# Two attentions and two feed-forward blocks on one core: the first batch in an order written out by hand, and pooling moved from VectorE to GpSimd

## The chip, the cores and the metric

The kernel runs on one core of a Trainium2 chip. The metric is the device time of one execution in microseconds (us); lower is better. Engines are named as the profile names them: PE is TensorE (matmul), DVE VectorE, ACT ScalarE, POOL GpSimd, SP the queue that issues most DMAs.

## What is computed

From q, k, v of shape (4 batches, 8 heads, 576, 64), all in float32:

```python
# pooled attention: 4 neighbours averaged, full softmax over 144
q_d = q.reshape(B, H, 144, 4, D).mean(axis=3)      # k_d, v_d alike
out_up = np.repeat(sm_attn(q_d, k_d, v_d), 4, axis=2)
# local attention: a row sees the rows less than 4 away (7 at most)
scores = np.where(np.abs(pos[:, None] - pos[None, :]) < 4, scale * q @ k.T, -1e9)
x = out_up + softmax(scores) @ v                   # as (2304 tokens, 512)
h = np.maximum(np.maximum(x @ w1, x @ w2), x @ w3) # 512 -> 768
x = h @ w_out                                      # 768 -> 512
h = x @ w_in                                       # 512 -> 2048
out = np.maximum(0.01 * h, h) @ w_out2             # 2048 -> 512
```

## The kernel before

The tokens are cut into 8 units u of 288 (NCOL), two to a batch. A program first computes the x of a unit (both attentions) and then its first feed-forward block. The second feed-forward block follows for all tokens, in 5 chunks (L3 and L4); the change leaves it alone.

**Feed-forward of a unit.** `L1_mm(u, m, e)` is 12 matmuls: x and the weights are each split into a high and a low part (xh, xl; a weight's two halves), and three products are summed, high by high first, then xl by high, then xh by low. 18 of these (6 m, 3 e) and then 4 `L2(u, o)` of 18 matmuls make a unit's PU = 22 slots. `L1_post` takes the maximum over e (hm) and splits it in hh (ACT) and hl (POOL).

**Weights.** `split_weight` turns a float32 weight into two parts by two ACT passes (wy, wl), two DVE passes on integers, one more ACT pass (high) and one subtraction (low, on POOL at first, later on DVE). The first block has 24 weights of 128x512. 14 of them (AHEAD) are converted during the first batch's attention, the others during u = 0.

**First batch (units 0 and 1).** Both attentions run on PE, four head pairs h. Pooled attention goes through `ds_pool_qk` (pooling q and k by 4, DVE), `ds_scores` (scores, maximum, exp, reciprocal of the sum), `ds_norm` (POOL), `ds_at` (transposes and copies) and `ds_pv`. Local attention goes through `pl_scores` (blocks of 96 rows by 102 columns; a band of very negative numbers is added first, by a matmul with an identity), `pl_aT`, `pl_pv` and `pl_x`, which adds both and writes xh and xl. `pl_pool_v` pools v on POOL. Unit 0's steps are a list of ten steps per head pair, each head pair one step behind the last; unit 1's are spread over the first 9 slots (U1) of u = 0. `keep_warm` puts matmuls on zeros, 20 at the start and 40 after the list.

**Other batches.** Pooled attention keeps these steps; `ds_stages` spreads seven stages of a head pair over slots (table in the loop over b). Local attention works on 128 rows at a time without PE: an item i is half the heads of a unit, so a unit u needs the items 2u and 2u+1. Each item has 3 chunks c: `qk_mult` (POOL, 128x1344), `qk_reduce` (DVE and ACT), then, one item later, `pv_mult` and `pv_sum` (DVE) into the tile O. The products of POOL and of DVE share one tile name, prod, with three buffers. From slot 9 on, the pieces of local attention are dealt evenly to the slots of L1, and `emit_T(u + 1)`, in the second L2 slot of u, transposes O (ps_x, PE), adds the pooled part (x, DVE) and makes xh (ACT) and xl (DVE) for the next unit.

**Order.** Only SP's order is that of the program text (`manual_schedule(engines={SP})`). On every other engine a scheduler orders the instructions when the program is built; on the chip each engine then works its list off strictly in that order.

Of the kernel before, what the change touches and what calls it, by code (L numbers as in the profile page):

```python
# [43 lines left out]
U1 = 9  # L44
AHEAD = 14
NA = 8
NWARM = (20, 40)
# [5 lines left out]
def local_global_attention_moe_kernel(  # L53
# [69 lines left out]
    for edge in (None, "first", "last"):  # L123
        bd = sup.tile([QB, KB], BF16, name=f"band_{edge}")
        P.memset(bd, 0.0)
        conds = [(1, -1, 0), (-1, 1, KB - QB)]
        if edge == "first":
            conds.append((1, 0, -(FAC - 1)))
        if edge == "last":
            conds.append((-1, 0, KB - FAC))  # L130
        for step, cm, base in conds:
            P.affine_select(
                out=bd, in_=bd, pattern=[[step, KB]], base=base, channel_multiplier=cm,
                compare_op=ALU.is_ge, fill=-(2.0**33),
            )
        bands.append(bd)

# [10 lines left out]
    def split_weight(raw, stage, lo_engine):  # L148
# [7 lines left out]
        A.activation(out=l3, in_=low16, func=AF.Copy, scale=2.0**-13, bias=-0.5 + 2.0**-14)  # L156
        V.scalar_tensor_tensor(  # L157
            out=l3, in0=high, scalar=-(2**31), in1=l3, op0=ALU.bitwise_and, op1=ALU.bitwise_or
        )
        V.scalar_tensor_tensor(  # L160
            out=y, in0=y, scalar=3, in1=l3, op0=ALU.logical_shift_left, op1=ALU.bitwise_or
        )
        r = pool.tile([128, 1024], F32R, tag=name, bufs=1, name=name)
        hi, lo = r[:, 0:512], r[:, 512:1024]
        A.activation(out=hi, in_=y.bitcast(F32), func=AF.Copy)
        lo_engine.tensor_tensor(out=lo, in0=y.bitcast(F32), in1=hi.bitcast(F32), op=ALU.subtract)
        return hi, lo
# [16 lines left out]

    def conv_w1(t):
        r = split_weight(wr.pop(t), mmp, P if 1 not in pools else V)
        if t[0] == "A":
            wA[t[1:]] = r
        else:
            wO[t[1]] = r  # L190
# [151 lines left out]
    def pl_load(what, h):  # L342
# [8 lines left out]
        elif what in "01":  # L351
            t = sup.tile([KB, NBLK, 128], F32, tag="sv" + what, bufs=4, name="sv" + what)
            nc.sync.dma_start(out=t.rearrange("p n d -> p (n d)"), in_=vW[0, int(what), h])
        else:
            t = late_tile([QC, 2, 2, FAC, D], "dsrawv")
# [4 lines left out]
    def pl_pool_v(h):  # L360
        raw = dst.pop((0, h, "vr"))
# [6 lines left out]
    def pl_scores(u, h, hh):  # L368
        qr, kr = pl[h, "q"], pl[h, "k"]
        pst = ps_early.tile([QB, 512], F32, tag="early", name="ps_ls")  # L370
        ps = pst[:, : NBLK * KB].rearrange("p (n k) -> p n k", n=NBLK)
        st = pst[:, NBLK * KB :]
        rows = slice(64 * hh, 64 * hh + 64)
# [12 lines left out]
        if hh == 0:
            if u == 0:
                pl[u, h, "e"] = late_tile([QB, 2, NBLK, KB], "ple")
            else:
                pl[u, h, "e"] = sup.tile([QB, 2, NBLK, KB], F32, tag="ple", bufs=2, name="ple")  # L390
        e = pl[u, h, "e"][:, hh]
        for j in range(NBLK):
            A.activation(
                out=e[:, j], in_=ps[:, j], func=AF.Exp, scale=SCALE,
                bias=nm[:, j : j + 1], accum_out=sm[:, j : j + 1],
            )
        if hh == 1:
            e, sm = pl[u, h, "e"], pl.pop((u, h, "sum"))
            sp = st[:, NBLK : 3 * NBLK].rearrange("p (x n) -> p x n", x=2)
            V.tensor_scalar(out=sp, in0=sm, scalar1=1e-9, scalar2=None, op0=ALU.add)  # L400
            V.reciprocal(out=sm, in_=sp)
            for x in range(2):
                (P if u == 0 else V).tensor_tensor(
                    out=e[:, x], in0=e[:, x], in1=sm[:, x].unsqueeze(2).to_broadcast((QB, NBLK, KB)), op=ALU.mult
                )

    def pl_aT(u, h):
# [23 lines left out]
    def pl_x(u, h):  # L431
# [38 lines left out]
    def ds_pool_qk(b, h):  # L470
# [10 lines left out]
    def ds_scores(b, h, hh):  # L481
        t = dst[b, h, "qk"]
        if hh == 0:
            if b:
                dst[b, h, "e"] = small(b, [QC, 2, 2, SD], "dse")
            dst[b, h, "sum"] = pools[b].tile([QC, 4], F32, tag="dssum", bufs=2, name="dssum")
        pst = ps_at.tile([QC, 512], F32, tag="at", name="ps_sc")
        ps = pst[:, : 2 * SD].rearrange("p (c s) -> p c s", c=2)
        st = pst[:, 2 * SD : 2 * SD + 2]
        rows = slice(64 * hh, 64 * hh + 64)  # L490
        for c in range(2):
            T.matmul(out=ps[:, c, :], lhsT=t[rows, 0, c * QC : c * QC + QC], rhs=t[rows, 1, :], start=True, stop=True)
        nm = pools[b].tile([QC, 2], F32, tag="dsnm", bufs=2, name="dsnm")
        V.tensor_reduce(out=st, in_=ps, axis=AX.X, op=ALU.max, negate=True)
        V.tensor_scalar(out=nm, in0=st, scalar1=SCALE / 16.0, scalar2=None, op0=ALU.mult)
        e, sm = dst[b, h, "e"], dst[b, h, "sum"]
        for c in range(2):
            A.activation(
                out=e[:, hh, c, :], in_=ps[:, c, :], func=AF.Exp, scale=SCALE / 16.0,
                bias=nm[:, c : c + 1], accum_out=sm[:, 2 * hh + c : 2 * hh + c + 1],  # L500
            )
        sm, sp = sm[:, 2 * hh : 2 * hh + 2], pst[:, 2 * SD + 2 : 2 * SD + 4]
        V.tensor_scalar(out=sp, in0=sm, scalar1=1e-9, scalar2=float(FAC), op0=ALU.add, op1=ALU.mult)
        V.reciprocal(out=sm, in_=sp)
# [444 lines left out]
```

## Time and profile before

| | |
|---|---|
| three timed runs | 913.1, 913.62 and 914.03 us, median 913.62 |
| the profiled execution | 914.8 us, its span 913.0 us |
| PE busy | 860.4 us, 94% |
| DVE, ACT, POOL busy | 526.8, 412.8 and 247.7 us |
| mean granted clock of PE | 0.932 |
| DMA | 75.13 MB, mean 82 GB/s |

The span is what the profile shows from the first instruction to the last; the execution's own time has 1.8 us more around it. [...]

### The profile page before, as it was taken

Reading aid. Unit: us, or ns where it says so; the run is one execution under the profiler, and the core shown is the slowest. Engines: PE = TensorE matmul, PEld = TensorE weight load, DVE = VectorE, ACT = ScalarE, POOL = GpSimd, SP = SyncE. Lnnn points to the kernel's source line nnn. Section 1 sums busy time; section 2 is a strip of 40 time slices with the busy share of each in tenths; the row PEclk is TensorE's granted clock in tenths of the full one; section 3 lists DMA queues with packets and bytes.
Section 4 is the critical chain, followed back from the end, with each engine's and each line's share of the span. In section 5 each row is a group of like instructions: output and inputs, shape, how many; then the busy total and the mean of one; then the engine's idle time right before and its main releaser. Section 6 shows DMA issues by size and latency. Waiting matters only on the chain.

```text
span 913.0 us, 13518 instructions
## 1 busy us (share of the span) xinstructions
PE 860.4 (94%) x4912; PEld 754.7 (83%) x4914; DVE 526.8 (58%) x919; ACT 412.8 (45%) x1537; POOL 247.7 (27%) x195
## 2 busy tenths in 40 slices
PE   8799988997989989799999999999999999999995
PEld 4478888996978979699999888888887888788894
DVE  3587888887968696777475699242223322322321
ACT  2664754655647456572274687232223222222221
POOL 3553539764755566350111000000000000000000
PEclk9555979897999999799999999999999999999998
DMA  8700624442423133112062920020003000200000
GB/s 219 269 1 24 254 72 147 167 135 70 136 95 122 33 122 111 48 46 73 1 235 105 355 120 1 0 93 1 1 0 93 1 1 2 68 1 1 19 29 23
DMA packets 30132, 75.13 MB, mean 82 GB/s; under 512 B 3267, under 2 KB 8691, under 8 KB 30067
## 3 DMA queue, kind: packets, MB, share of 16 engines
q1 hardware_dynamic: 25459, 69.56, 22.8%
q10 hardware_dynamic: 4608, 4.72, 1.5%
q8 instruction: 38, 0.62, 0.3%
q14 instruction: 27, 0.22, 0.1%
HBM read 64.83 MB, written 9.44 MB: 81 GB/s over the span
## 4 chain that ended last, share of the span: by engine, by line
PE 74%; DVE 12%; DMA 7%; issue 2%; ACT 2%; SPq 1%; POOL 1%; ACTq 0%; POOLq 0%; DVEq 0%
PE ps_h L614 21%; PE acc L717 20%; PE ps_g L693 20%; PE ps_o L644 5%; DMA raw<-x2d 2%; PE ps_up L531 2%; DVE O L298 2%; DVE xl L602 2%; DMA wA<-in_wa_dram 2%; PE ps_ls L379 2%; PE ps_lo L426 1%; DMA sv<-in_vW_dram 1%; DVE wl L157 1%; DVE wy L160 1%; DVE x L594 1%
## 5 line engine op out<-in xcount | busy, mean ns | idle before, releaser
L614 PE MATMUL ps_h<-xh,wA 128*128 128x288 f32 x1152 | 204.5, 311 | 6.3 <-ACT xh L601 3.1
L614 PEld LDWEIGHTS ps_h<-xh,wA 128*128 128x128 f32 x1152 | 177.9, 201 | 9.2 <-ACT xh L601 3.3
L717 PE MATMUL acc<-w2o,gh 128*128 128x512 f32 x576 | 178.2, 391 | 0.9 <-ACT gh L704 0.9
L693 PE MATMUL ps_g<-x2h,w2i 128*128 128x512 f32 (+1 forms) x640 | 158.9, 370 | 0.0
L701 DVE TENSOR_TENSOR g<-g,ps_g 128x512 f32<-128x512 f32 (+1 forms) x80 | 50.7, 634 | 184.0 <-ACT g L700 183.9
L693 PEld LDWEIGHTS ps_g<-x2h,w2i 128*128 128x128 f32 x640 | 114.6, 188 | 22.9
L700 ACT ACTIVATE g<-ps_g 128x512 f32<-128x512 f32 (+1 forms) x80 | 44.3, 553 | 185.2 <-PE ps_g L693 185.1
L614 PE MATMUL ps_h<-xl,wA 128*128 128x288 f32 x576 | 116.5, 308 | 10.7 <-DVE xl L602 10.7
L717 PEld LDWEIGHTS acc<-w2o,gh 128*128 128x128 f32 x576 | 106.8, 188 | 23.7 <-ACT gh L704 1.8
L247 POOL TENSOR_TENSOR qkprod<-lq,lk 128x1344 f32<-128x1344 f32 x36 | 112.0, 3120 | 42.6 <-DVE O L298 25.6
L717 PE MATMUL acc<-w2o,gl 128*128 128x512 f32 x288 | 112.2, 391 | 0.1
L614 PEld LDWEIGHTS ps_h<-xl,wA 128*128 128x128 f32 x576 | 93.2, 199 | 12.9 <-DVE xl L602 11.9
L260 ACT ACTIVATE qkprod<-qkprod 128x64 f32<-128x64 f32 x364 | 87.6, 245 | 24.2 <-POOL qkprod L247 23.8
L693 PE MATMUL ps_g<-x2l,w2i 128*128 128x512 f32 (+1 forms) x320 | 79.6, 370 | 0.0
L644 PE MATMUL ps_o<-hh,wO 128*128 128x288 f32 x384 | 77.4, 298 | 0.0
L705 DVE TENSOR_TENSOR gl<-g,gh 128x512 fp32r<-128x512 f32 (+1 forms) x80 | 51.0, 638 | 39.6 <-ACT gh L704 35.1
L260 ACT ACTIVATION_READ_ACCUMULATOR qkprod<-qkprod 128x1 f32 x364 | 69.6, 191 | 0.0
L704 ACT ACTIVATE gh<-g 128x512 fp32r<-128x512 f32 (+1 forms) x80 | 47.1, 588 | 42.6 <-DVE g L701 42.2
L693 PEld LDWEIGHTS ps_g<-x2l,w2i 128*128 128x128 f32 x320 | 56.8, 188 | 10.9
L635 POOL TENSOR_TENSOR hl<-hm,hh 128x288 fp32r<-128x288 f32 x48 | 40.9, 854 | 88.3 <-ACT hh L634 84.7
L717 PEld LDWEIGHTS acc<-w2o,gl 128*128 128x128 f32 x288 | 54.1, 188 | 12.6 <-DVE gl L705 0.9
L631 DVE TENSOR_TENSOR hm<-hm,ps_h 128x288 f32<-128x288 f32 x96 | 42.3, 445 | 32.8 <-PE ps_h L614 26.9
(124 smaller groups left out, 1216.2 us busy)
## 6 DMA issues: line engine op xcount, KB each, us to landing
wA<-in_wa_dram SPq DMA_DIRECT2D x18, 512.0 KB
w2i<-in_w_in_dram SPq DMA_DIRECT2D x16, 512.0 KB
w2o<-in_w_out_dram SPq DMA_DIRECT2D x16, 512.0 KB
lv<-in_vL_dram SPq DMA_DIRECT2D x12, 480.0 KB
lk<-in_k_dram SPq DMA_DIRECT2D x11, 480.0 KB
dsrawv<-in_vP_dram SPq DMA_DIRECT2D x16, 288.0 KB
x2d<-ev ACTq DMA_DIRECT2D x32, 144.0 KB
raw<-x2d SPq DMA_DIRECT2D x16, 256.0 KB
```

Source lines behind the costliest of these rows:

```text
L247: P.tensor_tensor(out=pr, in0=in0, in1=in1, op=ALU.mult)
L260: A.activation(out=pr[:, r, j], in_=pr[:, r, j], func=AF.Copy, accum_out=sc[:, r, j : j + 1])
L614: T.matmul(out=ps, lhsT=wA[m, e][wi][:, kk * 128 : kk * 128 + 128], rhs=xx[:, kk] if u < PEU else xx[:, :, kk, :], start=n == 0, stop=n == ...
L631: V.tensor_tensor(out=t, in0=t, in1=ps, op=ALU.max)
L635: P.tensor_tensor(out=hl[:, m], in0=t, in1=hh[:, m].bitcast(F32), op=ALU.subtract)
L644: T.matmul(out=ps, lhsT=wO[m][wi][:, os_], rhs=xx[:, m], start=n == 0, stop=n == 3 * M1 - 1)
L693: T.matmul(out=ps, lhsT=w2i[m][wi][:, kk * 128 : kk * 128 + 128], rhs=xx[:, kk, :n], start=j == 0, stop=j == 3 * KC - 1,)
L700: A.activation(out=g, in_=ps, func=AF.Copy, scale=0.01)
L701: V.tensor_tensor(out=g, in0=g, in1=ps, op=ALU.max)
L704: A.activation(out=gh, in_=g, func=AF.Copy)
L705: V.tensor_tensor(out=gl, in0=g, in1=gh.bitcast(F32), op=ALU.subtract)
L717: T.matmul(out=accs[c, t], lhsT=a[:, ts], rhs=w, start=m == 0 and j == 0, stop=m == M2 - 1 and j == 2)
```

## The change

One table (ORDER) sets the order of the first batch on PE, DVE, ACT and POOL; after it the scheduler orders them again. Each step of the pooled and the PE-side local attention is cut into functions of one engine each, named by letters (A is pooling, B, F, G, J, K, M, m, N, v pooled attention, C, D, E, H, I, O, o, P, Q, R, S local attention, L the pooling of v, w x y z u a weight's load and its four conversion steps). Only 8 weights are converted in it, the others follow one per slot of u = 0, all low parts on POOL. Matmuls on zeros (`fill`) stand ahead of most PE steps. A pair of head halves is issued alternately, and one band matmul of 306 columns takes the place of three of 102. `wl3` of these weights lies in PSUM. Unit 1's attention takes slots 0 to 14, local attention of the other batches starts at slot 15 (U1), DONE and TURN set by which slot it ends and where `emit_T` stands (3 to 9 slots ahead of the unit's L1), DS0 and DSOFF where the pooled stages stand. O has two buffers. For batches 1 to 3, q and k are pooled by two additions on POOL, and xl is made on POOL. The loads of v for pooling have 80 rows in place of 72, those for the first batch's local attention 112 in place of 102, the added rows being zeros.

```diff
-U1 = 9
-AHEAD = 14
+U1 = 15
+QP = 80
+KP = 112
+ORDER = (
+    "C0 A0 A1 L0 B0 D0 A2 C1 E0 L1 F0 B1 H0 G0 D1 I0 x0 C2 J0 L2 F1 E1 y0 K0 G1 D2 O0 L3 H1 E2 J1 M0 "
...
+FILL = {"B": 1, "C": 1, "O": 2, "M": 2, "N": 2, "P": 2}
+FILL0 = 20
+FILL1 = 8
+DONE = {2: 39, 3: 59, 4: 79, 5: 100, 6: 121, 7: 142}
+TURN = {2: 41, 3: 62, 4: 82, 5: 103, 6: 124, 7: 145}
+DS0 = {1: (15, 18, 21, 24), 2: (27, 38, 49, 60), 3: (68, 79, 90, 101)}
+DSOFF = {1: (0, 2, 5, 8, 6, 7, 11, 13), 2: (0, 5, 6, 9, 10, 11, 16, 20), 3: (0, 5, 6, 9, 10, 11, 16, 20)}
...
-        l3 = stage.tile([128, 512], I32, tag="wy", bufs=4, name="wl3")
+        l3 = (stage.tile([128, 512], I32, tag="wy", bufs=4, name="wl3") if ps is None else ps()).bitcast(I32)
...
-            O[u] = pools["att"].tile([128, RU, 128], F32, tag="O", bufs=1, name="O")
+            O[u] = pools["att"].tile([128, RU, 128], F32, tag="O", bufs=2, name="O")
...
-            t = sup.tile([KB, NBLK, 128], F32, tag="sv" + what, bufs=4, name="sv" + what)
+            t = sup.tile([KP, NBLK, 128], F32, tag="sv" + what, bufs=4, name="sv" + what)
...
-            V.tensor_reduce(out=t[:, j], in_=dst.pop((b, h, w)), axis=AX.X, op=ALU.add)
+            raw = dst.pop((b, h, w))
+            if b == 0:
+                V.tensor_reduce(out=t[:, j], in_=raw, axis=AX.X, op=ALU.add)
+            else:
+                P.tensor_tensor(out=raw[:, :, 0:2], in0=raw[:, :, 0:2], in1=raw[:, :, 2:4], op=ALU.add)
+                P.tensor_tensor(out=t[:, j], in0=raw[:, :, 0], in1=raw[:, :, 1], op=ALU.add)
...
             A.activation(out=xhf, in_=x32f, func=AF.Copy)
-            V.tensor_tensor(
+            P.tensor_tensor(
                 out=xl[:, g0:g1].rearrange("p r a g -> p (r a g)"), in0=x32f, in1=xhf.bitcast(F32), op=ALU.subtract
             )
...
+    with tc.manual_schedule(engines={ET.SP, ET.PE, ET.DVE, ET.Activation, ET.Pool}):
...
+        fill("", scratch(0, "", "warm_ps"), FILL0)
+        for w in ORDER.split():
+            n = int(w[1])
+            if w[0] in "xyzu":
+                conv_step(W1[n])
+            elif w[0] == "L":
+                pl_pool_v(n)
+            else:
+                if w == "O0":
+                    fill("", scratch(0, "", "warm_ps"), FILL1)
+                steps[w[0]](0, n)
...
+    with tc.manual_schedule(engines={ET.SP}):
...
+        for b in range(1, B):
+            for h in range(4):
+                for off, f in zip(DSOFF[b], ds_stages(b, h)):
+                    at(DS0[b][h] + off, f)
+        for u in range(PEU, NU):
+            at(TURN[u], lambda u=u: emit_T(u))
...
-                    if s == NS + 1 and not last and u + 1 >= PEU:
-                        emit_T(u + 1)
```

**The first batch on PE.** Before, one group of scores of the first batch stands like this (ps_ls are the local scores of one head half, its band and its product for each of three blocks):

```order
L376 MATMUL ps_ls<-band_first,ident_b 96x102
L379 MATMUL ps_ls<-skr,sqr 96x102
L376 LDWEIGHTS ident_b
L376 MATMUL ps_ls<-band_None,ident_b 96x102
L379 MATMUL ps_ls<-skr,sqr 96x102
```

Now the same part of the list has matmuls on zeros (warm) ahead of each step, and both head halves of a pair follow one another (x6):

```order
L166 MATMUL ps_lt<-warm 128x512
L484 MATMUL ps_lt<-ident,ple 102x96 x6
L166 LDWEIGHTS warm
L166 MATMUL ps_ls<-warm 128x512
L421 LDWEIGHTS ident_b
L421 MATMUL ps_ls<-band_108,ident_b 96x306
```

A pair's six band matmuls have become two, and 40 matmuls on zeros stand between the steps, beside 20 at the start and 8 ahead of the first transposes.

**POOL ahead of unit 2's L1.** Before, POOL's list around the end of unit 1 reads (dsrawv and dsv pool v, dse is the normalization, qkprod the local scores' products, hl the low part of h):

```order
L635 TENSOR_TENSOR hl<-hm,hh 128x288
L466 TENSOR_TENSOR dsrawv<-dsrawv 72x4x128
L635 TENSOR_TENSOR hl<-hm,hh 128x288 x2
L509 TENSOR_TENSOR dse<-dse,dssum 72x576
L247 TENSOR_TENSOR qkprod<-lq,lk 128x1344
L467 TENSOR_TENSOR dsv_2372<-dsrawv 72x256
```

Now the list up to unit 2's xl ends like this (dsraw and dsqk pool q and k; the xl of the last row is the first piece of unit 2's):

```order
L291 TENSOR_TENSOR qkprod<-lq,lk 128x1344
L565 TENSOR_TENSOR dsraw<-dsraw 128x144x2 x2
L550 TENSOR_TENSOR dsv_2078<-dsrawv 72x256
L291 TENSOR_TENSOR qkprod<-lq,lk 128x1344
L566 TENSOR_TENSOR dsqk<-dsraw 128x144 x2
L291 TENSOR_TENSOR qkprod<-lq,lk 128x1344
L549 TENSOR_TENSOR dsrawv<-dsrawv 72x4x128
L618 TENSOR_TENSOR dse<-dse,dssum 72x576
L726 TENSOR_TENSOR xl<-x_2253,xh 128x512
```

From the first pooling of q to this xl, POOL's list has 14 qkprod, as many as before up to the same place, and in addition the poolings of q and k; xl stands behind all of them.

**PE at the same place.** Now the end of unit 1 and the start of unit 2 read:

```order
L651 MATMUL ps_up<-aT,dsv_1974 128x144 x4
L577 MATMUL ps_sc<-dsqk 72x144 x4
L697 MATMUL ps_x<-ident,O 128x128 x9
L738 MATMUL ps_h<-xh,wA_0_439 128x288 x4
L738 MATMUL ps_h<-xh,wA_1_454 128x288 x4
L738 MATMUL ps_h<-xh,wA_2_605 128x288 x4
L738 MATMUL ps_h<-xh,wA_0_640 128x288 x4
L629 MATMUL ps_aT<-ident,dse 72x72 x8
L651 MATMUL ps_up<-aT,dsv_2078 128x144 x4
L577 MATMUL ps_sc<-dsqk 72x144 x2
L738 MATMUL ps_h<-xl,wA_0_439 128x288 x4
```

As before the change, four groups of L1 take their xh products first, and the first xl product waits for POOL now, where it waited for DVE.

## Rows read from the trace of the kernel before

**Rows 1.** Busy time by stage: from, to, length; busy us of PE, PEld, DVE, ACT, POOL; clock
```profile
0.00:90.50 90.50, 80.04 (x343) 55.76 (x346) 55.63 (x127) 46.61 (x158) 43.06 (x62) 0.64 0.42 129
90.50:137.80 47.30, 42.43 (x278) 40.01 (x278) 39.94 (x72) 29.66 (x73) 21.93 (x19) 0.86 0.44 165
137.80:222.40 84.60, 75.92 (x531) 71.33 (x529) 69.41 (x124) 43.93 (x256) 63.55 (x36) 0.90 0.38 124
222.40:275.30 52.90, 48.15 (x345) 47.01 (x345) 44.40 (x73) 32.61 (x208) 32.53 (x19) 0.94 0.36 118
275.30:504.20 228.90, 215.95 (x1597) 212.26 (x1598) 161.91 (x276) 119.64 (x593) 86.60 (x60) 0.97 0.28 91
504.20:913.00 408.80, 397.91 (x1824) 328.31 (x1823) 155.46 (x251) 140.37 (x252) 0.00 (x0) 0.99 0.13 44
```

**Rows 2.** Timeline of PE: start, us, instruction; first matmul of L1, and a wait
```profile
90.51 0.59 PE L614 MATMUL ps_h<-xh,wA 128*128 128x288 f32 x1
...
222.38 0.83 PE L614 MATMUL ps_h<-xl,wA 128*128 128x288 f32 x4 [2.38 <-DVE xl L602]
```

**Rows 3.** Timeline of PE in the first batch: matmuls on zeros, then one block's band and scores
```profile
31.36 3.19 PE L784 MATMUL warm_ps<-warm 128*128 128x512 bf16 x7 [0.22 <-issue]
...
85.21 0.32 PE L376 MATMUL ps_ls<-band_None,ident_b 96*96 96x102 bf16 x1
85.46 0.65 PE L379 MATMUL ps_ls<-skr,sqr 64*96 64x102 f32 x2
```

**Rows 4.** DMA from 8 to 15 us, then from 26 to 36 us (weights): packets, rate
```profile
DMA packets 641, 1.44 MB, mean 205 GB/s; under 512 B 70, under 2 KB 179, under 8 KB 641
...
DMA packets 1109, 4.04 MB, mean 404 GB/s; under 512 B 127, under 2 KB 127, under 8 KB 1108
```

**Rows 5.** Timeline of DVE: its first pooling
```profile
3.67 0.75 DVE L478 TENSOR_REDUCE dsqke<-sqr 128x144 f32<-128x576 f32 x1 [2.53 <-DMA sqr<-in_qT_dram]
```

**Rows 6.** Groups on DVE: busy us, mean ns of one | idle before
```profile
L384 DVE TENSOR_REDUCE ps_ls<-ps_ls 96x3 f32<-96x306 f32 x16 | 7.5, 473 | 7.5 <-PE ps_ls L379 7.5
L442 DVE TENSOR_TENSOR x<-ps_lo,up 64x288 f32<-64x288 f32 x16 | 7.2, 453 | 0.5
L504 DVE RECIPROCAL dssum<-ps_sc 72x2 f32<-72x2 f32 x32 | 4.5, 156 | 0.2
L157 DVE SCALAR_TENSOR_TENSOR wl<-wA,wl 128x512 int32<-128x512 int32 x18 | 20.9, 1161 | 11.4 <-ACT wl L156 11.3
L157 DVE SCALAR_TENSOR_TENSOR wl<-w2i,wl 128x512 int32<-128x512 int32 x16 | 10.9, 686 | 3.6 <-ACT wl L156 3.6
```

**Rows 7.** Groups on POOL from 137.8 to 222.4 us
```profile
L247 POOL TENSOR_TENSOR qkprod<-lq,lk 128x1344 f32<-128x1344 f32 x14 | 43.3, 3108 | 2.5 <-DVE O L298 2.4
L466 POOL TENSOR_TENSOR dsrawv<-dsrawv 72x512 f32<-72x512 f32 x5 | 6.4, 1280 | 13.8 <-DMA dsrawv<-in_vP_dram 13.8
L635 POOL TENSOR_TENSOR hl<-hm,hh 128x288 fp32r<-128x288 f32 x8 | 6.4, 805 | 0.3 <-ACT hh L634 0.2
L509 POOL TENSOR_TENSOR dse<-dse,dssum 72x576 f32<-72x576 f32 x4 | 4.6, 1144 | 0.5 <-DVE lp L279 0.5
L467 POOL TENSOR_TENSOR dsv<-dsrawv 72x256 f32<-72x256 f32 x5 | 3.6, 730 | 2.9 <-PE ps_up L531 2.7
```

**Rows 8.** Groups over the whole span: xl on POOL and on DVE, low weight parts, pooling on DVE
```profile
L166 POOL TENSOR_TENSOR wA<-wy,wA 128x512 fp32r<-128x512 f32 x18 | 24.9, 1384 | 23.7 <-ACT wA L165 22.1 <-issue 1.4
L602 DVE TENSOR_TENSOR xl<-x,xh 128x512 fp32r<-128x512 f32 (+3 forms) x18 | 19.9, 1116 | 4.5 <-ACT xh L601 4.5
L478 DVE TENSOR_REDUCE dsqk<-dsraw 128x144 f32<-128x576 f32 x24 | 17.6, 745 | 7.5 <-DMA dsraw<-in_qT_dram 5.9 <-DMA dsraw<-in_kT_dram 1.6
L448 POOL TENSOR_TENSOR xl<-x,xh 128x288 fp32r<-128x288 f32 x8 | 9.0, 1122 | 18.2 <-ACT xh L447 18.2
```

**Rows 9.** Longest waits of POOL from 137.8 to 275.3 us: us in total, times, longest
```profile
POOL dsrawv L466 <- DMA dsrawv<-in_vP_dram: 23.3, 6, 5.8
POOL qkprod L247 <- DVE O L298: 12.5, 3, 6.2
```

More of the change, by code (lines that the diff above doesn't have):

```diff
@@ L165, in split_weight @@
         A.activation(out=hi, in_=y.bitcast(F32), func=AF.Copy)
+        yield
         lo_engine.tensor_tensor(out=lo, in0=y.bitcast(F32), in1=hi.bitcast(F32), op=ALU.subtract)
-        return hi, lo
+        yield hi, lo
+    def split_weight(raw, stage, lo_engine):
+        return list(split_steps(raw, stage, lo_engine))[-1]
     def x32_tile(n):
@@ L183, in load_w1, with conv_step @@
         wr[t] = load_weight(src, wpool, "w" + t[0] + "_".join(map(str, t[1:])))
-    def conv_w1(t):
[L186 to L190, printed above, removed]
+    conv = {}
+    def conv_step(t):
+        if t not in conv:
+            conv[t] = split_steps(wr.pop(t), mmp, P, lambda: scratch("0" not in PS, "mm", "wl3"))
+        r = next(conv[t])
+        if r and t[0] == "A":
+            wA[t[1:]] = r
+        elif r:
+            wO[t[1]] = r
+        return r
+    def conv_w1(t):
+        while not conv_step(t):
+            pass
     HS = S * D
@@ L366, in pl_pool_v, with pl_C @@
         dst[0, h, "v"] = v32
-    def pl_scores(u, h, hh):
+    def pl_C(u, h):
         qr, kr = pl[h, "q"], pl[h, "k"]
[L370 to L373, printed above, removed]
+        n = NBLK * KB
+        pst = pl[u, h, "ps"] = [scratch(u, "early", "ps_ls") for hh in range(2)]
+        if u == 0:
+            fill("C", pst[0])
+        for t in pst:
+            T.matmul(
+                out=t[:QB, :n], lhsT=ident_b, rhs=bands[u].rearrange("p n k -> p (n k)"), start=True, stop=False
+            )
@@ new lines, in pl_H, with pl_I @@
+    def pl_H(u, h):
+        st, sm = pl.pop((u, h, "st")), pl[u, h, "sum"]
+        pl.pop((u, h, "ps"))
+        for hh in range(2):
+            sp = st[hh][:, NBLK : 2 * NBLK]
+            V.tensor_scalar(out=sp, in0=sm[:, hh], scalar1=1e-9, scalar2=None, op0=ALU.add)
+            V.reciprocal(out=sm[:, hh], in_=sp)
+    def pl_I(u, h):
+        e, sm = pl[u, h, "e"], pl.pop((u, h, "sum"))
+        P.tensor_tensor(out=e, in0=e, in1=sm.unsqueeze(3).to_broadcast((QB, 2, NBLK, KB)), op=ALU.mult)
@@ L502, in ds_scores @@
-        sm, sp = sm[:, 2 * hh : 2 * hh + 2], pst[:, 2 * SD + 2 : 2 * SD + 4]
-        V.tensor_scalar(out=sp, in0=sm, scalar1=1e-9, scalar2=float(FAC), op0=ALU.add, op1=ALU.mult)
-        V.reciprocal(out=sm, in_=sp)
+        pst = dst[b, h, "ps"] = [scratch(b, "at", "ps_sc") for hh in range(2)]
+        if b == 0:
+            fill("B", pst[0])
+        for c in range(2):
+            for hh in range(2):
+                rows = slice(64 * hh, 64 * hh + 64)
+                T.matmul(
+                    out=pst[hh][:QC, c * SD : c * SD + SD], lhsT=t[rows, 0, c * QC : c * QC + QC],
+                    rhs=t[rows, 1, :], start=True, stop=True,
+                )
@@ L506, in ds_norm, with ds_J @@
+    def ds_J(b, h):
+        st, sum4 = dst.pop((b, h, "st")), dst[b, h, "sum"]
+        dst.pop((b, h, "ps"))
+        for hh in range(2):
+            sm = sum4[:, 2 * hh : 2 * hh + 2]
+            V.tensor_scalar(out=st[hh][:, 2:4], in0=sm, scalar1=1e-9, scalar2=float(FAC), op0=ALU.add, op1=ALU.mult)
+            V.reciprocal(out=sm, in_=st[hh][:, 2:4])
     def ds_norm(b, h):
```

395 lines of the change are left out of this document (202 added, 193 removed), and 3 rows, old and new, of the table ORDER.

## The prediction

> **What bounds the kernel now.** I read the busy time by stage first, then PE's timeline at the stage borders, then the groups and waits of the engine that ends each stage. The last stage, the second feed-forward block, is 408.8 us with PE busy for 397.9 [rows 1]; the change has no line in it, so it stays. The 504.2 us ahead of it fall into three parts. Until 90.5 us the first batch's attention runs and no matmul of L1 has started [rows 2]; PE is busy for 80.0 us of that, but at a mean granted clock of 0.64 [rows 1]. From 137.8 to 275.3 us (unit 0's end, unit 1, unit 2) PE is busy for 124.1 of 137.5 us while DVE is busy for 113.8 and POOL for 96.1 [rows 1]: units 2 and 3 wait for local attention, and the last wait is DVE's xl [rows 2]. From 275.3 to 504.2 us PE is busy for 216.0 of 228.9 us [rows 1], so this part is close to PE's own work.
>
> **First batch, 0 to the first L1.** Two things can set its end after the change. DVE's work: in its new list up to the last x of unit 0 there are 8 poolings of 0.75 us [rows 5], 16 row maxima and 8 copies of about 0.47 and 8 additions of 0.45 [rows 6], 4 copies of a pooled result (taken at 0.3), 48 instructions on a few columns of about 0.156 [rows 6], and 16 passes over 8 weights. A pass took 1.161 us while POOL worked beside it and 0.686 when POOL was idle [rows 6]; now one of its operands lies in PSUM, and I take the lower price, since what made it dear was POOL's company. That gives 6.0 + 11.3 + 3.6 + 1.2 + 7.5 + 11.0 = 40.6 us; at the dear price 48. DVE starts at 3.67 us [rows 5] and will wait some 6 us for the first head pairs, which makes 50 us the lower end. ACT was busy for 46.6 us of the 90.5 [rows 1] with more weights and half of unit 1's scores in it, so it is not the later one.
>
> The other is PE. At the lower clock level a matmul on zeros took 3.19/7 = 0.46 us, a band 0.32 and a block's scores 0.65 [rows 3]. From the 80.0 us of busy time I take off unit 1's scores, half of which were done in this stage (4 head halves of 3 x 0.93 = 2.8 us, 11 us), and the saved bands (about 4 us), and add 8 more matmuls on zeros (3.7 us): 69 us if the clock stays where it was, and with some 6 us of waits 75, the upper end. At the higher level it is about half, and DVE decides. The new matmuls on zeros stand between the steps, so the clock may be at the higher level part of the time, but the rows cannot say how much. I take the middle, 62 us, so 28.5 us sooner than 90.5. The padded loads belong here: from 8 to 15 us, with loads of 72 and 102 rows among them, the DMA engines moved 205 GB/s, with 128-row weights 404 GB/s [rows 4]. At the better rate the 4.4 MB that the first batch needs, and the first weights, land by about 17 us; at the old rate some 9 us later, which stays inside 50 to 75.
>
> **Unit 0 until local attention starts.** POOL's list has all 24 low parts, of 1.384 us [rows 8], of which 16 are now in unit 0. In 90.5 to 137.8 us (47.3 us, [rows 1]) 10 weights and most of unit 1's attention stood. Now 16 weights and all of unit 1's attention stand there, but the clock is up from the start (before, 0.86), and DVE's passes are cheaper. I take 48 us, between 42 (the PE work without waits) and 56 (the weights at the dear price). Local attention's loads wait for the tiles of the first batch, so POOL's first qkprod of batch 1 has its start at 62 + 48 = 110 us, against 137.8.
>
> **Units 1 and 2, the term that takes back.** Pooling q and k (DVE, 0.745 us each [rows 8]) and xl go to POOL. I count POOL's new list from the first pooling to unit 3's xl: 24 qkprod of 3.108, 13 hl of 0.805, 9 and 8 additions for v of 1.280 and 0.730, 7 normalizations of 1.144 [rows 7], 20 first additions of 288 columns, 18 second ones of 144, and two xl of 1152 columns. The new ones have no row. The nearest for 288 columns are 0.805 [rows 7] and 1.122 [rows 8]; I take 0.85, since DVE loses work beside it. For 144 I take 0.45, between half of 0.805 and the 0.730 of 256 columns. An xl is 3.1 us at 1.384 per 512 columns. So 74.6 + 10.5 + 17.4 + 8.0 + 17.0 + 8.1 + 6.2 = 142 us without a wait, 136 to 153 at the ends of the two prices. The same stretch was 137.5 us before. So POOL is the bound here: xl of unit 2 stands behind 14 qkprod and all of batch 1's poolings. I add 8 us of waits (before, POOL's qkprod waited 12.5 us for DVE and its pooling of v 23.3 us for loads [rows 9]; the loads are now issued earlier, and DVE has less to do) and get 150 us, unit 3's xl at 260 us against 275.3. So of the 27.8 us gained until here 12.5 are given back.
>
> [...]
>
> **Units 3 to 7.** PE's busy time, 216.0 us [rows 1], is what stays if the waits go. They were waits for x and xl; emit_T now stands 4 to 9 slots ahead of its unit instead of 3, and POOL had 86.6 us of work in these 228.9 us [rows 1], some 20 more with the last poolings and four xl at the prices above, so it has room. I take 216; the ends are 214 and 229.
>
> **Sum.** 260 + 216 + 408.8 = 884.8 us of span; the profiled execution had 1.8 us around it and lay 1.2 us above the median, so **885 us** against 913.62.
>
> **Rivals.** (1) The clock stays at the lower level through the first batch. For it: 0.64 in the stage although PE was busy for 88% of it [rows 1]. Against it: the matmuls on zeros ahead of each step. L1 then starts at 75, and the time is 898. [...] (2) The first batch runs at DVE's pace and POOL's list goes through without a wait: 50 + 48 + 142 + 216 + 408.8, 865 us. For it: DVE's 40.6 us are all that is left once PE is at the higher level. (3) Slower: POOL's strict list idles as it did. From 137.8 to 222.4 us it was busy for 63.55 of 84.6 us, 75% [rows 1], waiting for buffers and loads in turn. If the new list keeps that share, 142 us of work take 190 and unit 3's xl comes at 300: 925 us. It decides from 178 us on, a busy share of 80%. For it: qkprod still shares three buffers with DVE's products, and norms wait for ACT and DVE. Against it: the loads that made up most of that idle time are issued earlier.
>
> **Chances.** My forecast 0.52, (1) 0.15, (2) 0.18, (3) 0.15, of which 0.04 ends near no change. So faster by over 0.2% (about what a measurement can tell here) 0.85, within it 0.04, slower 0.11. The range reaches from a little below (2), where the low price of pooling is added, to just under no change: 857 to 910 us. The forecast's own is 872 to 898.
>
> **What would show it.** Right: the first L1 matmul near 62 us, POOL over 90% busy from about 110 to 260 us, PE waiting for an xl of L726 before units 2 and 3 and hardly later, 216 us from unit 3's xl to the first ps_g, the last 409 us the same. Wrong: POOL idle for more than 30 us in its stretch (then 3), a first L1 past 75 us, or the waits for xl still there at units 4 to 7.

## Result and the profile after

The changed kernel takes **885.61 us** (median of 4 runs, 883.63 to 889.43). The kernel before, on the same chip, took 913.83 (913.1 to 914.65). The ratio is 0.9696, 95% interval 0.9662 to 0.973, so 28 us faster. The forecast was 885. The profiled execution took 885.25 us with a span of 883.4.

The same view as [rows 1], busy time by stage, with the changed kernel's own borders: first L1 matmul, GpSimd's first pooling for batch 1, first L1 of units 2 and 3, first ps_g (at 474.33 us; the row is drawn at 474.50). Columns as there.

```profile
0.00:57.30 57.30, 42.68 (x303) 28.42 (x307) 39.48 (x110) 36.32 (x126) 35.20 (x52) 0.87 0.81 265
57.30:101.50 44.20, 43.44 (x327) 41.02 (x326) 36.67 (x91) 37.93 (x108) 32.44 (x31) 0.97 0.24 88
101.50:193.80 92.30, 70.02 (x480) 64.27 (x478) 68.31 (x114) 42.60 (x252) 79.17 (x65) 0.81 0.43 144
193.80:250.70 56.90, 52.76 (x354) 50.15 (x354) 50.22 (x82) 38.01 (x256) 50.72 (x40) 0.89 0.37 119
250.70:474.50 223.80, 218.59 (x1605) 214.26 (x1606) 140.01 (x234) 114.11 (x546) 94.43 (x79) 0.97 0.22 73
474.50:883.40 408.90, 397.89 (x1824) 328.39 (x1823) 155.50 (x251) 140.41 (x252) 0.00 (x0) 0.99 0.14 50
```

The first L1 comes 33 us sooner than before, and the last stage is what it was. The third row is the weak one: PE idles for 22 of 92 us, and no engine is busy for more than 86%. PE's timeline (start, us, instruction, idle time before it and what ended it) tells where:

```profile
55.67 0.41 PE L421 MATMUL ps_ls<-band,ident_b 96*96 96x306 bf16 x1 [6.45 <-DVE wy L190]
...
57.28 0.61 PE L738 MATMUL ps_h<-xh,wA 128*128 128x288 f32 x1
...
179.81 1.09 PE L697 MATMUL ps_x<-ident,O 128*128 128x128 f32 x4 [6.51 <-DVE ps_sc L612]
...
193.82 4.21 PE L738 MATMUL ps_h<-xh,wA 128*128 128x288 f32 x16 [10.91 <-ACT xh L725]
...
265.64 1.33 PE L738 MATMUL ps_h<-xh,wA 128*128 128x288 f32 x4 [3.99 <-ACT hm L752]
```

The longest wait, 10.91 us, is for xh of unit 2, so for ScalarE, and ScalarE had itself waited for VectorE's x. VectorE's timeline over those microseconds:

```profile
181.18 1.14 DVE L718 TENSOR_TENSOR x<-ps_x,up 128x256 f32<-128x256 f32 x2
182.24 6.57 DVE L310 TENSOR_TENSOR ls<-ls,mask 128x21 f32<-128x21 f32 x1
188.74 1.54 DVE L342 TENSOR_REDUCE O<-pvprod 128x192 f32<-128x1344 f32 x1
190.20 1.54 DVE L301 TENSOR_REDUCE ls<-qkprod 128x21 f32<-128x1344 f32 x1
191.66 0.21 DVE L314 TENSOR_REDUCE lp<-ls 128x9 f32<-128x63 f32 x1
191.78 1.41 DVE L718 TENSOR_TENSOR x<-ps_x,up 128x256 f32<-128x256 f32 x3
...
193.11 0.17 DVE L310 TENSOR_TENSOR ls<-ls,mask 128x21 f32<-128x21 f32 x1
```

L310 takes the minimum of 21 columns with a mask. It took 0.17 us at 193.11 and 6.57 us at 182.24, and the rest of unit 2's x stood behind it. GpSimd's timeline beside it:

```profile
180.96 3.03 POOL L291 TENSOR_TENSOR qkprod<-lq,lk 128x1344 f32<-128x1344 f32 x1
183.95 1.26 POOL L549 TENSOR_TENSOR dsrawv<-dsrawv 72x512 f32<-72x512 f32 x1
185.16 1.14 POOL L618 TENSOR_TENSOR dse<-dse,dssum 72x576 f32<-72x576 f32 x1
186.27 1.26 POOL L726 TENSOR_TENSOR xl<-x,xh 128x512 fp32r<-128x512 f32 x1
187.49 1.29 POOL L565 TENSOR_TENSOR dsraw<-dsraw 128x288 f32<-128x288 f32 x2
193.64 1.69 POOL L726 TENSOR_TENSOR xl<-x,xh 128x512 fp32r<-128x512 f32 x2 [4.87 <-ACT xh L725]
```

The minimum started while GpSimd multiplied, and ended at 188.81 us, 0.03 us after GpSimd's last pooling (188.78), when GpSimd had nothing to do. Most of the other held minima were held for less: one that started at 110.55 us ended at 113.46, 0.04 us after the multiplication that was running, although GpSimd went on at once. Both operands of L310 lie in SBUF. Every other VectorE instruction of this stretch reads at most one from there. The groups over the whole span (busy us, mean ns of one | idle before):

```profile
L310 DVE TENSOR_TENSOR ls<-ls,mask 128x21 f32<-128x21 f32 x12 | 23.1, 1924 | 0.9 <-ACT qkprod L304 0.9
...
L565 POOL TENSOR_TENSOR dsraw<-dsraw 128x288 f32<-128x288 f32 x24 | 15.6, 670 | 0.9 <-DMA dsraw<-in_qT_dram 0.9
...
L187 DVE SCALAR_TENSOR_TENSOR wl<-wA,wl 128x512 int32<-128x512 int32 x18 | 12.3, 689 | 5.2 <-ACT wl L185 5.1
...
L726 POOL TENSOR_TENSOR xl<-x,xh 128x512 fp32r<-128x512 f32 x9 | 11.5, 1284 | 16.2 <-ACT xh L725 16.2
...
L566 POOL TENSOR_TENSOR dsqk<-dsraw 128x144 f32<-128x144 f32 x24 | 10.3, 454 | 1.8 <-PE ps_sc L577 1.8
```

The twelve minima took 23.1 us. A pass over a weight (L187) is at 0.689 us, and GpSimd's new additions took 0.670 and 0.454 us, a 512-column xl 1.284. The group of the minima in the kernel before, where GpSimd was busy for 75% of the comparable stretch [rows 1]:

```profile
L266 DVE TENSOR_TENSOR ls<-ls,mask 128x21 f32<-128x21 f32 x12 | 8.3, 688 | 5.5 <-ACT qkprod L260 5.5
```

The profile also follows the work that ended last back from instruction to releaser. From 101 to 254 us this chain holds no GpSimd instruction, and three of the minima, 13.2 us together (start, us):

```profile
110.64 2.82 DVE ls L310
...
182.32 6.50 DVE ls L310
...
242.57 3.87 DVE ls L310
```

This gave a second theory. **A**, the prediction's: from 101 to 254 us GpSimd's amount of work is the bound. **B**: VectorE is held in instructions with two SBUF operands until GpSimd lets it in.

### The profile page after: what moved, and what is told of

Read it like the earlier page. It is cut to its first block, busy times and chain, and to the rows that moved or that the text cites. A ratio compares the mean times of both kernels' runs of the same rounds, so it can differ in the third digit from the quotient of the medians.

```text
span 883.4 us, 13548 instructions
## 1 busy us (share of the span) xinstructions
PE 825.4 (93%) x4886; PEld 726.5 (82%) x4890; DVE 490.2 (55%) x880; ACT 409.4 (46%) x1537; POOL 292.0 (33%) x263
## 4 chain that ended last, share of the span: by engine, by line
PE 84%; DVE 6%; DMA 4%; ACT 3%; issue 1%; SPq 1%; ACTq 0%; DVEq 0%
PE ps_h L738 26%; PE acc L841 21%; PE ps_g L817 21%; PE ps_o L768 8%; DMA raw<-x2d 2%; PE ps_up L651 2%; DVE ls L310 2%; PE ps_sc L577 2%; ACT qkprod L304 2%; PE ps_lo L504 1%; PE ps_aT L629 1%; DMA skr<-in_kTp_dram 1%; PE ps_ls L429 1%; DVE x L718 1%; DVE pvprod L335 1%
## 5 line engine op out<-in xcount | busy, mean ns | idle before, releaser
L738 PE MATMUL ps_h<-xh,wA 128*128 128x288 f32 x1152 | 201.5, 306 | 17.9 <-ACT xh L725 10.9
L738 PEld LDWEIGHTS ps_h<-xh,wA 128*128 128x128 f32 x1152 | 172.4, 195 | 22.6 <-ACT xh L725 11.4
L738 PE MATMUL ps_h<-xl,wA 128*128 128x288 f32 x576 | 113.6, 303 | 0.0
L738 PEld LDWEIGHTS ps_h<-xl,wA 128*128 128x128 f32 x576 | 90.9, 194 | 0.8 <-issue 0.8
L768 PE MATMUL ps_o<-hh,wO 128*128 128x288 f32 x384 | 75.3, 296 | 0.0
```

What stands on the lines that cost most here:

```text
L738: T.matmul(out=ps, lhsT=wA[m, e][wi][:, kk * 128 : kk * 128 + 128], rhs=xx[:, kk] if u < PEU else xx[:, :, kk, :], start=n == 0, stop=n == ...
L768: T.matmul(out=ps, lhsT=wO[m][wi][:, os_], rhs=xx[:, m], start=n == 0, stop=n == 3 * M1 - 1)
```

## Experiments

The kernel before had medians of 915.5 to 916.5 us in the runs that follow, against 913.83 above, so versions are compared by their ratio to it. The changed kernel's is 0.9696 (0.9662 to 0.973).

**1. The mask through PSUM.**
```diff
-        V.tensor_tensor(out=sl, in0=sl, in1=masks[half], op=ALU.min)
...
         pb = pools["s"].tile([128, n + 2 * RU], F32, tag="lp", name="lp")
...
+        V.tensor_copy(out=pr[:, 0:RC, :], in_=sl)
+        V.tensor_tensor(out=sl, in0=pr[:, 0:RC, :], in1=masks[half], op=ALU.min)
```


> The edit: the scores' border rows are copied into PSUM first and the minimum with the mask reads that copy, so this VectorE instruction has one operand in SBUF instead of two (twelve copies of 21 columns more). Theory A, the prediction's (from 101 to 254 us GpSimd's amount of work is the bound): the minimum may get shorter, but GpSimd's list and unit 3's last xl stay within 2 us of 253.7 us, time 884 to 887. Theory B (a VectorE instruction with two SBUF operands is held until GpSimd pauses; the minimum took 0.17 to 6.57 us, 23.1 us in all, and the longest one stands just ahead of the x for which TensorE waited 10.9 us at unit 2): all twelve minima take under 0.3 us, TensorE's wait for xh at unit 2 falls from 10.9 to under 6 us, unit 3's xl comes 5 to 9 us sooner, time 873 to 880.

Measured 870.38 us, ratio 0.9506 (0.9484 to 0.9528), 2.0% below the changed kernel and a little below the range of theory B. VectorE's timeline at the same place:

```profile
179.47 1.14 DVE L719 TENSOR_TENSOR x<-ps_x,up 128x256 f32<-128x256 f32 x2
180.52 0.17 DVE L313 COPY lp<-ls 128x21 f32<-128x21 f32 x1
180.61 1.54 DVE L343 TENSOR_REDUCE O<-pvprod 128x192 f32<-128x1344 f32 x1
182.07 1.54 DVE L301 TENSOR_REDUCE ls<-qkprod 128x21 f32<-128x1344 f32 x1
183.53 0.17 DVE L314 TENSOR_TENSOR ls<-lp,mask 128x21 f32<-128x21 f32 x1
183.62 1.42 DVE L719 TENSOR_TENSOR x<-ps_x,up 128x256 f32<-128x256 f32 x3
```

All twelve minima now take 0.17 to 0.18 us. From one L719 to the next it is 4.1 us instead of 10.6, unit 3's last xl ends at 244.5 instead of 253.7, and the first ps_g comes at 460.9 instead of 474.3. GpSimd's work was not touched, and no minimum is left in the chain of this stretch. So GpSimd's amount of work was not what set the stretch as it stood, and B holds.

The changed kernel's trace also shows what ended most of the holds: seven of the nine minima of over 0.3 us ended within 0.1 us of the end of the GpSimd instruction that was running when they started, as the one at 110.55 us did. Two did not: at 242.50 us the minimum (3.94 us) was held past the multiplication that was running and past one more GpSimd instruction, at 182.24 us (6.57 us) past five more; no run shows why.

**2. xl back on VectorE**, both operands in SBUF.
```diff
-            P.tensor_tensor(
+            V.tensor_tensor(
                 out=xl[:, g0:g1].rearrange("p r a g -> p (r a g)"), in0=x32f, in1=xhf.bitcast(F32), op=ALU.subtract
```


> The edit: xl of units 2 to 7 goes back from GpSimd to VectorE, everything else as in the changed kernel. Theory A (GpSimd's amount of work is the bound): its list loses 18 subtractions of about 1.0 to 1.3 us, two units' worth (6 us) ahead of unit 3's L1, time 876 to 884. Theory B (VectorE with two SBUF operands is held while GpSimd works): the 18 subtractions take over 1.1 us in the mean and some over 3 us, against 0.3 to 0.7 us by their width, and the x behind them come late; time 888 to 900.

Measured 879.76 us, 0.9616 (0.958 to 0.9653), 0.8% below the changed kernel. The group of the widest:

```profile
L726 DVE TENSOR_TENSOR xl<-x,xh 128x512 fp32r<-128x512 f32 x9 | 9.0, 998 | 0.7 <-ACT xh L725 0.7
```

The mean is 0.998 us against 0.68 without a hold (experiment 10), the longest 2.28: the hold is there, and the minima took 27.9 us in all, more than before this edit. Yet the time went down, as A had it, and B's range was missed. This run's trace doesn't show why: it was the slowest of six (886.41; the others 874.68 to 885.19), and its first ps_g came at 475.5 us, as late as the changed kernel's. The cause of this gain stays open.

**3. Pooling of q and k back on VectorE.**
```diff
-            if b == 0:
+            if True:
                 V.tensor_reduce(out=t[:, j], in_=raw, axis=AX.X, op=ALU.add)
```


> The edit: pooling of q and k for batches 1 to 3 goes back to VectorE as one reduction of 576 columns each (0.75 us), in place of two additions on GpSimd (0.65 and 0.44 us). Theory A: GpSimd's list until unit 3's xl gets 20 us shorter and that xl comes 8 to 15 us sooner; time 870 to 879. Rival (VectorE, busy for 88% of the stretch ahead of unit 3, becomes the bound with 15 us more): unit 3's xl as late as now or later, time 885 to 895.

Measured 871.35 us, 0.9513 (0.9491 to 0.9534), 1.9% below. Unit 3's xl ends at 243.1 us. The number is A's, but the minima had fallen from 23.1 to 16.4 us at the same time. They do not account for the gain: the longest still stood ahead of unit 2's x, as long as before:

```profile
175.96 6.89 DVE L310 TENSOR_TENSOR ls<-ls,mask 128x21 f32<-128x21 f32 x1
```

Until unit 3's xl the held minima were only some 4 us shorter in all, while that xl came 10.6 us sooner. Experiment 7 tests the two together.

**4. The PSUM banks in another order**, against the wait of 6.45 us before the first L1.
```diff
+    scratch(0, "", "wl3")
     stats = PS["0"].tile([128, 512], F32, tag="st", bufs=1, name="stats")
...
-        PS["mm"] = p1.enter_context(tc.tile_pool(name="ps_mm", bufs=4, space=PSUM, reuse_waits="tile"))
         PS["at"] = p1.enter_context(tc.tile_pool(name="ps_at", bufs=2, space=PSUM, reuse_waits="tile"))
+        PS["mm"] = p1.enter_context(tc.tile_pool(name="ps_mm", bufs=4, space=PSUM, reuse_waits="tile"))
```


> The edit: the PSUM banks are handed out in another order, so that the bank of the weight conversion's scratch goes to a pool that is used later, and not to unit 1's second score tile. Theory (that bank alone held TensorE for 6.45 us ahead of the first L1, and the gain stays): first L1 matmul at 50 to 52 us instead of 57.28, and 4 to 6 us less at the end, 880 to 882. Rival 1 (the gain is given back: in the stretch up to unit 3 VectorE and GpSimd end as late as now): first L1 at 51, time 884 to 887. Rival 2 (the weights themselves are the wait): TensorE then waits as long at L1's first weights or x, first L1's twelfth matmul no sooner, 885.

Measured 889.35 us, 0.9707 (0.9673 to 0.9741): no difference that shows. The first L1 did come at 50.81 us, but then PE waited for the conversion all the same:

```profile
59.70 0.61 PE L739 MATMUL ps_h<-xh,wA 128*128 128x288 f32 x1 [4.82 <-DVE wy L191]
```

Local attention's first multiplication came at 107.6 us instead of 104.3. So the gain of 6.5 us was lost inside unit 0, the second rival.

**5. No matmuls on zeros** (what is left out feeds no result).
```diff
-FILL = {"B": 1, "C": 1, "O": 2, "M": 2, "N": 2, "P": 2}
-FILL0 = 20
-FILL1 = 8
+FILL = {}
+FILL0 = 0
+FILL1 = 0
...
-        for _ in range(FILL[what] if n is None else n):
+        for _ in range(FILL.get(what, 0) if n is None else n):
```


> The edit: all 68 matmuls on zeros of the first batch are left out (they feed no result). Theory (they hold TensorE's clock up, as the prediction's rival 1 has it without them): the granted clock until the first L1 falls from about 0.88 towards 0.64, the first L1 comes at 65 to 75 us instead of 57.28, time 892 to 904. Rival (VectorE, ScalarE and the weights pace the first batch): first L1 within 2 us of 57, time 883 to 888.

Measured 894.26 us, 0.9768 (0.9736 to 0.98), 0.7% above the changed kernel, with the first L1 at 61.95 us, sooner than the 65 to 75 expected. From 34 to 46 us, the stretch's row (columns as in the stage table; the clock is the third number from the end), without the zeros:
```profile
34.00:46.00 12.00, 11.80 (x63) 10.72 (x60) 8.38 (x26) 8.04 (x31) 4.12 (x5) 1.00 0.24 68
```
Two groups of PE in it:
```profile
L504 PE MATMUL ps_lo<-plt,sv 102*128 102x96 f32 x19 | 4.5, 424 | 0.2 <-DVE plt L494 0.2
L651 PE MATMUL ps_up<-dsvaT 72*128 72x144 f32 x16 | 4.5, 460 | 0.0
```
The same two groups of the changed kernel, in the same stretch:
```profile
L504 PE MATMUL ps_lo<-plt,sv 102*128 102x96 f32 x24 | 3.1, 277 | 0.3 <-DVE plt L494 0.3
L651 PE MATMUL ps_up<-dsvaT 72*128 72x144 f32 x16 | 2.3, 285 | 0.0
```
And of the kernel before from 60 to 90 us, where the granted clock was 0.50:
```profile
L426 PE MATMUL ps_lo<-plt,sv 102*128 102x96 f32 x40 | 10.7, 423 | 0.0
L531 PE MATMUL ps_up<-dsvaT 72*128 72x144 f32 x32 | 8.9, 461 | 0.0
```

Without the zeros the matmuls of this stretch take what they took in the kernel before at a granted clock of 0.50 (424 and 460 ns against 423 and 461). The clock column reads 1.00 there, so it cannot be trusted in this run; the durations decide.

**6. The conversion's scratch back in SBUF.**
```diff
-            conv[t] = split_steps(wr.pop(t), mmp, P, lambda: scratch("0" not in PS, "mm", "wl3"))
+            conv[t] = split_steps(wr.pop(t), mmp, P)
```


> The edit: the scratch wl3 of the weight conversion goes back from PSUM into the shared SBUF buffers wy, as before the change. Theory B (two SBUF operands are held while GpSimd works): the passes over a weight take 1.0 to 1.3 us in the mean instead of 0.69, 24 weights of two passes cost 15 to 25 us of VectorE until 100 us, first L1 at 60 to 66 us, local attention starts 4 to 10 us later, time 889 to 897. Theory of the prediction's wording (GpSimd's company makes them dear wherever the operands lie): the passes now take 0.69 only because GpSimd is less busy, so they stay under 0.8 us and the time within 3 us of 885.

Measured 908.73 us, 0.9927 (0.9899 to 0.9956), 2.4% above and beyond either range: 21 us of the change's 28 are gone. Its groups of the two passes on VectorE, and the minimum:

```profile
L190 DVE SCALAR_TENSOR_TENSOR wy<-wy,wl 128x512 int32<-128x512 int32 x56 | 52.5, 939 | 0.8
...
L310 DVE TENSOR_TENSOR ls<-ls,mask 128x21 f32<-128x21 f32 x12 | 28.9, 2408 | 0.7 <-ACT qkprod L304 0.7
...
L187 DVE SCALAR_TENSOR_TENSOR wl<-wA,wl 128x512 int32<-128x512 int32 x18 | 21.2, 1177 | 3.1 <-ACT wl L185 3.0
...
L187 DVE SCALAR_TENSOR_TENSOR wl<-wO,wl 128x512 int32<-128x512 int32 x6 | 10.3, 1710 | 6.5 <-ACT wl L185 6.5
```

The first pass is back at 1.177 us, as before the change (1.161, [rows 6]), and GpSimd worked beside it in both kernels (busy for 35.2 of the first 57.3 us in the changed one, for 37.7 of 57 here). So where the operand lies decides, theory B. The first L1 came at 51.2 us here (no scratch bank to wait for) and the loss followed in unit 0: local attention's first multiplication came at 111.1 us, 7 us later than in the changed kernel. The edit also makes scratch and result share four buffers again; what of the 21 us that is was not separated.

**7. Experiments 1 and 3 together.**

> The edits of the first and the third experiment together: the minimum reads PSUM, and q and k are pooled on VectorE. If the two gains (15 and 14 us against the changed kernel) are separate, one from the held VectorE and one from GpSimd's shorter list: 855 to 860. If both are the same gain, the held minimum (which a shorter GpSimd list makes rarer): 867 to 872.

Measured **866.9 us**, 0.9477 (0.9444 to 0.9509), the lowest of all: 2.3% below the changed kernel and 5.2% below the one before. Of experiment 3's 1.9% only 0.3 points are left in the time once the minimum is free, and the intervals of 1 and 7 overlap: by the time, the two gains are in the main the same. The traces do not bear that out at unit 3's xl. It ended at 235.3 us, 18.5 sooner than in the changed kernel, against 9.2 sooner in experiment 1 and 10.6 in experiment 3, nearly their sum, and no minimum was held here. Then units 3 to 7 took 220.2 us, 3.8 more than in experiment 1. So taking the poolings off GpSimd does bring this stretch forward, beside the freed minimum; why the gain does not last to the end is not shown.

**8. No padding of the value loads.**
```diff
-QP = 80
-KP = 112
+QP = 72
+KP = 102
```


> The edit: the value loads go back to 72 and 102 rows. Theory (loads with fewer rows run at about half the rate): the 4.4 MB of the first batch land 5 to 9 us later, the first L1 comes at 60 to 66 us, later loads of 72 rows show up as GpSimd's wait for its pooling of v; time 887 to 895. Rival (the loads are hidden): first L1 within 2 us of 57, time 883 to 887.

Measured 887.19 us, 0.968 (0.9637 to 0.9722): no difference that shows, first L1 at 58.55 us instead of 57.28. The padded loads are hidden in time.

**9. Six weights in the first batch instead of eight**, on top of 7 (the steps x, y, z, u of weights 6 and 7 leave the order, and `ci` is 6).

> The edit, on top of the seventh experiment (mask through PSUM, q and k pooled on VectorE: 866.9): only six of the 24 weights are converted inside the first batch, the other eighteen in unit 0's slots. Theory (TensorE's 6.46 us wait for the eighth weight's scratch bank is a loss of its own): first L1 at 48 to 51 us instead of 55.6 and 3 to 6 us less in all, 861 to 864. Rival (as with the PSUM banks in another order: the wait comes back in unit 0, where the conversion of the weights then paces L1): first L1 at 50, but local attention's first product no sooner than 102, time 866 to 870.

Measured 869.04 us, 0.948 (0.9461 to 0.9499), the same as experiment 7. The first L1 came at 50.72 us, but local attention's first multiplication at 101.9 against 102.6. The row from there to 80 us:

```profile
50.70:80.00 29.30, 25.85 (x193) 23.38 (x192) 23.65 (x61) 28.15 (x80) 20.98 (x19) 0.94 0.43 176
```

ScalarE is busy for 28.15 of 29.30 us, with the conversions that no longer stood ahead. That fits experiment 4: around the first L1 the weights' passes seem to set the pace wherever they stand.

**10 and 11. xl on VectorE, on top of 7**, once read from the PSUM bank of x, once with both operands in SBUF.
```diff
-            x32 = x32_tile(n * 128).rearrange("p (r c) -> p r c", c=128)
+            x32 = pt
...
-            P.tensor_tensor(
+            V.tensor_tensor(
                 out=xl[:, g0:g1].rearrange("p r a g -> p (r a g)"), in0=x32f, in1=xhf.bitcast(F32), op=ALU.subtract
```
Experiment 11 has the second part alone.

> The edit, on top of the seventh experiment (866.9): x stays in its PSUM bank, and xl is taken from there on VectorE, so with one operand in SBUF; GpSimd has no xl any more. Theory (what xl cost on VectorE was the hold for two SBUF operands): the 18 subtractions take 0.3 to 0.7 us by their width with none above 0.8, unit 3's xl comes 2 to 4 us sooner, time 862 to 866. Rival (the PSUM banks, held longer by xl, hold up pooled attention's transposes, or VectorE has too much): 867 to 874.

> The edit, on top of the seventh experiment (866.9): xl goes back to VectorE with both operands in SBUF. Theory B (held while GpSimd works): several of the 18 subtractions take over 1.5 us, mean of the 512-column ones about 1.0, and the time is 2 to 6 us above the tenth experiment's. Rival (with GpSimd's list shorter by all poolings of q and k, it pauses often enough): mean under 0.75 us, time within 2 us of the tenth experiment's.

Measured 875.58 us, 0.9561 (0.9537 to 0.9585), and 870.82 us, 0.9486 (0.9459 to 0.9513). The widest group of experiment 10:

```profile
L727 DVE TENSOR_TENSOR xl<-ps_x,xh 128x512 fp32r<-128x512 f32 x9 | 6.1, 684 | 1.4 <-ACT xh L726 1.4
```
PE's two longest waits in it (us in total, times, longest):
```profile
PE ps_x L698 <- DVE xl L727: 11.3, 2, 6.6
PE ps_aT L630 <- DVE xl L727: 8.6, 3, 6.3
```
The same group of experiment 11:
```profile
L727 DVE TENSOR_TENSOR xl<-x,xh 128x512 fp32r<-128x512 f32 x9 | 9.5, 1056 | 1.1 <-ACT xh L726 1.1
```

The hold went away as B said (0.684 us, none above 0.69, against 1.056 with one of 3.98), but the time went up, beyond the rival's range too: two PSUM banks serve x and pooled attention's transposes, and kept longer they cost PE 20 us of waits, where experiment 7 had 2.6 us of waits for x. A cure for one resource was paid with another. Held subtractions, on the other hand, cost nothing measurable against experiment 7, so theory B missed the order of these two times. That fits a hold mattering only by what stands behind it, which no run tests by itself.

**12. Only k on VectorE, with the mask through PSUM.**
```diff
-            if b == 0:
+            if b == 0 or w == "k":
```


> The edit: the mask through PSUM as in the first experiment (870.38), and of batches 1 to 3 only k is pooled on VectorE, q stays on GpSimd. Theory (with the minimum no longer held, VectorE and GpSimd share the bound from 100 to 240 us, so the middle between them is best): 862 to 866, below both neighbours (870.38 with both on GpSimd, 866.9 with both on VectorE). Rival (a chain of waits through ScalarE and the transposes bounds that stretch, not an amount of work): between the two neighbours, 866 to 871.

Measured 869.86 us, 0.9504 (0.9482 to 0.9527): between its neighbours, as the rival had it. With the minimum free, where q and k are pooled hardly shows in the time. Unit 3's xl came at 248.4 us, later than in either neighbour (244.5 and 235.3), and the first ps_g at 459.2, between theirs (460.9 and 455.4). So neither engine's amount of work puts these runs in order, and the chain of waits that does was not taken apart.

## Why the prediction was right, and where it was not

The sum came out: 57.3 + 44.2 + 152.2 + 220.6 + 409.1 us against the forecast's 62 + 48 + 150 + 216 + 408.8. One term was right for a wrong reason.

- **First batch** (62, ends 50 and 75; measured 57.28): right in size. VectorE's work was 39.5 us where 40.6 were counted. The two clock levels that the prediction reckoned with are in the trace of the kernel before: at a granted clock of 0.50 a matmul on zeros took 0.46 us [rows 3], at 1.00, from 12.34 us on, 26 of them took 5.78 us, 0.22 each. But neither VectorE's amount nor the clock closed it. The last of the eight conversions did, by its PSUM scratch bank: 6.45 us, a wait that the sum didn't have. Experiments 4 and 9 show that it is worth nothing by itself: local attention started no sooner, or hardly, and the time did not fall.
- **The price of a pass**: the low one was right (0.689 us measured, 0.686 taken), the reason was not. "What made it dear was POOL's company" left out half the condition. With GpSimd beside it, it is dear with two SBUF operands (1.177, experiment 6) and cheap with one (0.689, the changed kernel). Had I kept to my reason, the dear price would have been the one to take, since GpSimd was busy for 35.2 of the 57.3 us. This edit carries up to 21 of the 28 us.
- **Padded loads**: taken as hidden inside the first batch's range; experiment 8 agrees.
- **Unit 0** (48; 44.2): right in size. The forecast's 110 us stood both for the first pooling (101.45) and for the first qkprod (104.26); counted to the latter it is 47.0.
- **Units 1 and 2** (150 until unit 3's xl; measured 152.2, from 101.45 to 253.7): the number fits by luck, and the step "so POOL is the bound here" fails. The durations in GpSimd's list add up to 136.4 us, not 142, mostly because an addition of 288 columns took 0.67 instead of 0.85. They overlap a little, so GpSimd was busy for 132.9 us, 87% and not over 90%. (The low end of that sum is 140 at the two low prices, not 136.) TensorE waited for xh, not for xl, and the chain of this stretch holds 13.2 us of minima and nothing of GpSimd. Experiment 1 left that list alone and took 9 us off the stretch. The overcharged list happened to stand in for held minima that the sum didn't contain. Taking the poolings off it brought unit 3's xl 9 to 11 us forward all the same (experiments 3 and 7), so what fails is GpSimd as the one bound.
- **Units 3 to 7** (216; 220.6): 4.6 us too low. Of TensorE's waits just after the start, the 3.99 us until 265.64 were for ScalarE, which had been reducing local attention's products; only the next, of 1.22 us, follows a minimum of 2.94 us, at 265.51. With the minima free the stretch took 216.4 us in experiment 1, the forecast's figure, but 220.2 in experiment 7, so the 4.6 us are not shown to be the minima's.
- **Last stage** (408.8; 409.1): unchanged, as said.

Of the rivals, the first (the clock stays low, 898) has its mechanism shown in experiment 5: without zeros the matmuls from 34 to 46 us take 424 and 460 ns, as at a granted clock of 0.50, and with them 277 and 285; the time is 894, though L1 starts at 62 and not at 75. With them the clock was 0.87 in the first batch, so it did not decide. Why the matmuls stay slow without them, although PE was busy for 11.8 of these 12 us, no run shows. The second (GpSimd's list without a wait, 865) names about the time of experiment 7, which got there by another way. The third, slower, did not come: GpSimd's share was 87%, above the 80% from which it decides.

## What to carry to other kernels

Before moving work to GpSimd, look for VectorE instructions with two operands in SBUF: in this kernel seven of the nine minima of over 0.3 us ended within 0.1 us of the end of the GpSimd instruction they had started beside, and beside a GpSimd that was busy for 87% of the stretch a minimum of 21 columns took up to 6.57 us. Look for such a hold in the chain: from 101 to 254 us three of the seven minima stood in it. Look at a group's longest instance, not only at its mean, and where a 21-column instruction took 6.57 us, compare its end with the other engine's. A sum of stages that comes out right does not show that the named bound was the bound; an edit that leaves that bound alone, and still moves the time, tells that it was not the only one.

## What was not expected of the hardware

- A VectorE minimum of 128 x 21 elements took between 0.17 and 6.57 us. With one operand in PSUM all twelve took 0.17 to 0.18.
- The longest was held not for one GpSimd instruction but for a run of them: it started at 182.24 us, and GpSimd's multiplication ended at 183.99, followed by five instructions up to 188.78. Seven of the nine minima that took over 0.3 us ended within 0.1 us of the end of the GpSimd instruction that was running when they started.
- The granted clock read 1.00 while matmuls took 424 and 460 ns, the durations of a stretch granted 0.50 (423 and 461).
